# Weight tiles padded from 4,096 to 4,160 bytes in a partition, in a kernel of chunked scan, gated and squared-ReLU layers

## The chip, the cores and the metric

The kernel runs on one core of a Trainium2 chip. The metric is the device time of one execution in microseconds (us). Five engines work on their own instruction lists: TensorE (PE for matmuls, PEld for loads of the stationary operand), VectorE (DVE), ScalarE (ACT), GpSimd (POOL) and SyncE (SP, which issues most DMAs here). They share SBUF, a memory of 128 partitions; a tile is a piece of it that starts at the same byte address in each partition.

## The reference

Three layers follow one another on 3,072 tokens (4 batches of 768) of width 256.

```
for c in range(nc):                       # scan: 8 heads of 32, state 16, chunks
    L  = exp(cum_i - cum_j) * causal
    y[c] = (C B^T * L) x + (C state) * exp(cum)
    state = exp(sum la) * state + sum_j B_j x_j * decay_from_j
x = y as 3072 x 256
g = x @ w_gate; val = x @ w_val           # 256 x 1536 each
x = (silu(g) * val) @ w_out               # 1536 x 256
h = x @ w_in                              # 256 x 2048
out = (relu(h) ** 2) @ w_out2             # 2048 x 256
```

The weights come in as 64-bit numbers and are turned into 32-bit ones on the chip.

## The kernel before, in words

Nearly every product is taken three times: each operand is split into a high and a low part in a rounded 32-bit format (fp32r), and hi·hi, hi·lo and lo·hi are added in PSUM. So a matrix product of two 128-row halves is six matmuls for a front (L791: `g`, `v` and `h`, with weights stationary and the activations `xh_all`, `xl_all` moving) and six for a back (L905, L977: `acc`, with weights stationary and the activation's parts `p` moving). In the last 512 tokens of the third layer the roles are exchanged (L986: 128 x 128 pieces of `p` are stationary, 256 columns of the weights move). A few early products are taken once in full 32 bits instead, from the unsplit weights `v` and the activations `xf` or `t`.

A `Unit` (L382) stands for 1,024 columns of weights. `load` brings them by DMA into `raw`; ACT, DVE and POOL make the 32-bit value `v` (`mag` L441, `share` L447, `sign` L456, `clamp` L462, `shift` L466), then ACT writes the high part `hi` (`top`, L472) and POOL or DVE the low part `lo` (`rest`, L476). `v`, `hi` and `lo` are tiles of 128 x 1,024 words, so 4,096 bytes in a partition. Those of the first two layers and of the last four units of the third come from the pool `w` of 20 tiles (L188); the first four units of the third layer use room that the scan has given up (the pools `xf`, `tr`, `L`, `ab`, L1105).

The order of all work is written out beforehand: `Graph.order` (L51) walks the tables in `PLAN["seq"]`, one list for each engine, and only the costs and tables there decide it, no address. `new` (L225) takes a tile from a pool when an operation that needs it is issued.

The pools lie in SBUF one behind another, in the order in which they are opened: fixed tiles (among them `xh_all`, `xl_all`, `xa`, `mt`), then `w`, `raw`, `tmp` (the tiles `t` and `o`), `p`, `tr`, `L`, `ab`, `xf`, `st`. In the built program `w` begins at byte 73,856 of a partition. Below, a tile's *place* is its byte address less whole multiples of 1,024. All 20 tiles of `w` begin at place 128, and so do `xh_all`, `xl_all`, `raw`, `t`, `p`, the tiles of `tr`, `L`, `ab`, and `xf`. An operand of a matmul is a piece of a tile: a stationary one of 128 words (512 bytes) begins at place 128 or 640, since pieces follow each other by 512 bytes.

Of the kernel before, what the change touches and what calls it, by code (L numbers as in the profile page):

```python
# [141 lines left out]
def kernel(  # L142
# [23 lines left out]
    P = 128  # L166
# [8 lines left out]
    for b in range(NB):  # L175
        t = 0
        while t < S:
            n = min(Q, S - t)
# [10 lines left out]
    tp = {  # L189
        k: ctx.enter_context(  # L190
            tc.tile_pool(name=k, bufs=v, space=PSUM) if k.startswith("ps") else tc.tile_pool(name=k, bufs=v)
        )
        for k, v in pools.items()
    }
# [30 lines left out]
    def new(buf, shape, dtype, tag=None):  # L225
        n = 1
        for d in shape[1:]:
            n *= d
        if buf.pool in ("L", "ab") and n < 1024:

            t = tp[buf.pool].tile([P, 1024], dtype, tag=buf.pool, name=tag or buf.pool)[:, :n]
            buf.t = t.rearrange("p (a b) -> p a b", a=shape[1]) if len(shape) == 3 else t
        else:
            buf.t = tp[buf.pool].tile(shape, dtype, tag=buf.pool, name=tag or buf.pool)
        if buf.pool == "ps" and fills:


            t = buf.t.rearrange("p a b -> p (a b)") if len(shape) == 3 else buf.t
            t = t[:, : min(n, 256)]
            for _ in range(fills.pop()):  # L240
                nc.tensor.matmul(t, idle[:, : shape[0]], idle[:, : t.shape[-1]], start=True, stop=True)  # L241
        return buf.t
# [139 lines left out]
    class Unit:  # L382
# [37 lines left out]
        def load(self, raw, s, src):  # L420
            if raw.t is None:
                new(raw, [P, 2, 1024], I32)
            w, rows, j = src
            if rows:
                v = w[256 * j : 256 * j + 256, :].rearrange("(i p) f -> p i f", p=P)
            else:
                v = w[:, 512 * j : 512 * j + 512].rearrange("(k p) f -> p k f", p=P)
            nc.sync.dma_start(out=raw.t[:, s].rearrange("p (i f) -> p i f", i=2), in_=v)
# [8 lines left out]
        def mag(self, raw, c):  # L437

            if self.v.t is None:
                new(self.v, [P, 1024], F32, "v")  # L440
            nc.scalar.activation(self.part(c), self.words(raw, c)[1].bitcast(F32), AF.Abs, scale=65536.0)  # L441
# [28 lines left out]
        def top(self):  # L470
            new(self.hi, [P, 1024], F32R, "hi")
            nc.scalar.activation(self.hi.t, self.v.t, AF.Copy)  # L472
# [594 lines left out]
    for i, (j, c0, c1, exact) in enumerate(PLAN["cells"]):  # L1067
        ti, o = (0, c0 * Q) if c0 < 3 else (1, c0 * Q - cut)
        n = min(c1 * Q, S) - c0 * Q
# [55 lines left out]
    with tc.manual_schedule():  # L1125
        for op in order:
            fills.clear()
            if op.eng == "PE":
                if op.start < PLAN["warm"]:
                    free = max([last] + [o.start + o.took + 250 for o in op.after if o is not None])  # L1130
                    gap = op.start - free
                    n = (gap - COLD) / 110 + COLD / 216 if free < 1200 else gap / 105
# [153 lines left out]
```

## Time and profile before

| | before |
|---|---|
| median of 2 runs | 627.29 us (627.07 and 627.5) |
| profiled execution, its own time | 627.6 us |
| its span, first to last instruction | 625.9 us |
| PE busy | 619.8 us (99%), 3,682 matmuls |
| DVE busy | 424.6 us (68%) |
| ACT busy | 335.2 us (54%) |
| POOL busy | 99.4 us (16%) |
| mean granted clock of TensorE | 0.999 |

The profile is of one execution. "Busy" is time in which an engine has an instruction in flight. Matmuls overlap their neighbours, and the end of one is modelled: a 512-column matmul is listed with 389 ns, while the next starts 227 ns after it. The distance from start to start is therefore what a matmul costs in a stream, and it is read from the chain of work or from the order of time. A span of x matmuls in the chain of work, divided by x, gives it.

### The profile page before, as it was taken

The numbers are of one execution on the slowest core, as the hardware profiler recorded it, in microseconds if no ns is written. First come the engines' busy times: TensorE is split into PE (matmuls) and PEld (weight loads), VectorE is DVE, ScalarE is ACT, GpSimd is POOL, SyncE is SP. The second block draws the span as 40 slices with busy tenths as digits, with TensorE's granted clock in tenths as the row PEclk, the third lists the DMA queues.
The fourth block names the chain that finished last, engine by engine and source line by source line (L and its number), as shares of the span: only waits on it lengthen the run. The fifth ranks groups of instructions, "written<-read, shape, count | busy, mean of one in ns | idle before, by whom it ended". The sixth has DMA issues, their size and how long they took to land.

```text
span 625.9 us, 9674 instructions
## 1 busy us (share of the span) xinstructions
PE 619.8 (99%) x3682; PEld 525.1 (84%) x3682; DVE 424.6 (68%) x668; ACT 335.2 (54%) x615; POOL 99.4 (16%) x130
## 2 busy tenths in 40 slices
PE   8999999999999999999999999999999999999997
PEld 6889999998878787878888888888888888888897
DVE  7897888877876866883688985454545554545543
ACT  6898985455443535542476564444444444444443
POOL 2425513313121231211113310000000000000000
PEclk9999999999999999999999999999999999999999
DMA  8879975756656555640224200010010100200101
GB/s 185 212 191 228 209 151 93 132 110 124 135 96 132 99 102 118 148 137 33 68 68 135 68 1 0 1 34 1 9 26 1 35 2 0 35 0 1 34 1 36
DMA packets 153855, 49.85 MB, mean 80 GB/s; under 512 B 141648, under 2 KB 142160, under 8 KB 153808
## 3 DMA queue, kind: packets, MB, share of 16 engines
q1 hardware_dynamic: 153248, 48.87, 35.4%
q8 instruction: 29, 0.48, 0.3%
q10 hardware_dynamic: 560, 0.36, 0.2%
q14 instruction: 18, 0.15, 0.1%
HBM read 34.96 MB, written 3.25 MB: 61 GB/s over the span
## 4 chain that ended last, share of the span: by engine, by line
PE 98%; DMA 1%; DVE 0%; SPq 0%; issue 0%; DVEq 0%
PE h L791 21%; PE g L791 18%; PE acc L977 17%; PE acc L905 16%; PE v L791 14%; PE acc L986 4%; PE ys L727 3%; PE cb L688 2%; PE cb L679 1%; PE ab L616 1%; DMA dv<-in_a_dram 1%; PE trb L529 0%; PE g L241 0%; PE cb L241 0%; PE turn L766 0%; PE ab L241 0%
## 5 line engine op out<-in xcount | busy, mean ns | idle before, releaser
L967 DVE TENSOR_TENSOR p<-t,p 128x512 fp32r<-128x512 f32 x96 | 68.2, 713 | 65.2 <-ACT p L963 65.2
L963 ACT ACTIVATE p<-t 128x512 fp32r<-128x512 f32 x96 | 60.6, 633 | 75.9 <-PE acc L977 53.3
L960 DVE TENSOR_TENSOR t<-t 128x512 f32<-128x512 f32 x96 | 66.2, 691 | 51.6 <-ACT t L957 51.6
L977 PE MATMUL acc<-p,hi 128*128 128x512 f32 x320 | 98.6, 389 | 0.0
L957 ACT ACTIVATE t<-h 128x512 f32<-128x512 f32 x96 | 57.4, 598 | 66.1 <-PE h L791 63.2
L905 PE MATMUL acc<-p,hi 128*128 128x512 f32 (+3 forms) x320 | 90.2, 366 | 0.0
L855 ACT ACTIVATE t<-g 128x512 f32<-128x512 f32 (+5 forms) x88 | 44.8, 516 | 71.9 <-PE g L791 63.9
L791 PE MATMUL h<-xh_all,hi 128*128 128x512 f32 x192 | 74.8, 390 | 0.0
L791 PE MATMUL h<-xl_all,hi 128*128 128x512 f32 x192 | 74.8, 390 | 0.0
L791 PE MATMUL h<-xh_all,lo 128*128 128x512 f32 x192 | 74.7, 389 | 0.0
L878 DVE TENSOR_TENSOR p<-t,p 128x512 fp32r<-128x512 f32 (+3 forms) x80 | 57.4, 727 | 21.0 <-ACT p L873 20.4
L873 ACT ACTIVATE p<-t 128x512 fp32r<-128x512 f32 (+3 forms) x80 | 45.4, 572 | 47.2 <-DVE t L858 38.6
L977 PEld LDWEIGHTS acc<-p,hi 128*128 128x128 f32 x320 | 60.1, 188 | 12.5
L858 DVE TENSOR_TENSOR t<-t,v 128x512 f32<-128x512 f32 (+2 forms) x68 | 43.7, 647 | 36.0 <-PE v L791 26.8
L791 PE MATMUL g<-xh_all,hi 128*128 128x512 f32 (+3 forms) x184 | 65.3, 355 | 0.0
L791 PE MATMUL g<-xl_all,hi 128*128 128x512 f32 (+3 forms) x184 | 64.6, 351 | 0.0
L791 PE MATMUL g<-xh_all,lo 128*128 128x512 f32 (+3 forms) x184 | 64.6, 351 | 0.0
L905 PEld LDWEIGHTS acc<-p,hi 128*128 128x128 f32 x320 | 57.1, 189 | 7.3
L977 PE MATMUL acc<-p,lo 128*128 128x512 f32 x160 | 62.2, 389 | 0.0
L905 PE MATMUL acc<-p,lo 128*128 128x512 f32 (+3 forms) x160 | 57.9, 362 | 0.0
L791 PE MATMUL v<-xh_all,hi 128*128 128x512 f32 (+2 forms) x136 | 51.2, 377 | 0.0
L791 PE MATMUL v<-xl_all,hi 128*128 128x512 f32 (+2 forms) x136 | 51.0, 375 | 0.0
(108 smaller groups left out, 1071.7 us busy)
## 6 DMA issues: line engine op xcount, KB each, us to landing
ab<-decay SPq DMA_DIRECT2D x23, 452.0 KB, 4.2
raw<-in_moe_w_out_dram SPq DMA_DIRECT2D x14, 512.0 KB, 5.5
raw<-in_moe_w_in_dram SPq DMA_DIRECT2D x8, 512.0 KB, 3.8
raw<-in_moe_w_val_dram SPq DMA_DIRECT2D x6, 512.0 KB, 5.2
raw<-in_moe_w_gate_dram SPq DMA_DIRECT2D x6, 512.0 KB, 5.4
xa<-in_x_dram SPq DMA_DIRECT2D x24, 112.0 KB, 3.0
out_dram<-o SPq DMA_DIRECT2D x40, 64.0 KB, 1.9
bc<-in_B_dram SPq DMA_DIRECT2D x18, 56.0 KB, 2.9
```

The source lines that it names most:

```text
L791: nc.tensor.matmul(ps, l, r, start=(i == 0), stop=(i == len(terms) - 1))
L855: nc.scalar.activation(t[:, :n], gg(), AF.Silu)
L858: nc.vector.tensor_tensor(tb.t[:, :n], tb.t[:, :n], vv(), op=ALU.mult)
L873: nc.scalar.activation(p[:, 0, :n], tb.t[:, :n], AF.Copy)
L878: e.tensor_tensor(p[:, 1, :n], tb.t[:, :n], p[:, 0, :n].bitcast(F32), op=ALU.subtract)
L905: nc.tensor.matmul(ps, l, r, start=bank not in done_f, stop=f == NF - 1, skip_group_check=True,)
L957: nc.scalar.activation(new(tb, [P, TN], F32, "t"), ph.t, AF.Relu)
L960: nc.vector.tensor_tensor(tb.t, tb.t, tb.t, op=ALU.mult)
L963: nc.scalar.activation(new(pb, [P, 2, TN], F32R, "p")[:, 0, :], tb.t, AF.Copy)
L967: e.tensor_tensor(pb.t[:, 1, :], tb.t, pb.t[:, 0, :].bitcast(F32), op=ALU.subtract)
L977: nc.tensor.matmul(acc[-1 - i][m], l.t[:, w], pb.t[:, r, :], start=(f == 0 and s == 0), stop=(f == NF2 - 1 and s == 2),)
L986: nc.tensor.matmul(acc[-1 - i][q][:, :256], pb.t[:, l, tk], r, start=(f == 0 and s == 0), stop=(f == NF2 - 1 and s == 2),)
```

## The change

A tile of pool `w` is taken with 1,040 words instead of 1,024, and the last 16 words (64 bytes) are cut off again. Each tile still has 1,024 words in use, at a distance of 4,160 bytes from the next one.

```diff
@@ new(buf, shape, dtype, tag=None) @@
             t = tp[buf.pool].tile([P, 1024], dtype, tag=buf.pool, name=tag or buf.pool)[:, :n]
             buf.t = t.rearrange("p (a b) -> p a b", a=shape[1]) if len(shape) == 3 else t
+        elif buf.pool == "w":
+            buf.t = tp["w"].tile([P, 1040], dtype, tag="w", name=tag or "w")[:, :n]
         else:
             buf.t = tp[buf.pool].tile(shape, dtype, tag=buf.pool, name=tag or buf.pool)
```

The two added lines move the line numbers behind them by two (L977 becomes L979). On every engine the list of instructions is otherwise the same row for row, in the same order, with the same tile numbers and sizes: no instruction, no DMA and no wait is added, removed or moved. Only addresses differ. The tiles of `w` begin at 73,856 + 4,160·i, so at places 128, 192, 256 and so on in steps of 64 bytes. These are 16 places for 20 tiles: the last four stand at the places of the first four. Everything behind `w` (`raw`, `t`, `o`, `p`, `tr`, `L`, `ab`, `xf`, `st`) lies 1,280 bytes higher, so at place 384 where it was at 128. What lies ahead of `w` (`xh_all`, `xl_all`, `xa`, `mt` and the other fixed tiles) stays.

Of the 2,688 matmuls in fp32r, 1,968 take a stationary operand from a tile of `w`, and 96 a moving one. 1,068 of the 1,968 take it from tiles that begin at an odd multiple of 64 bytes after the change: 756 of them with 512 moving columns, 112 with 432, 88 with 336 and 112 with 256.

## Rows read from the trace of the kernel before

**Rows 1.** The page's head: the span, and busy time of PE.

```profile
span 625.9 us, 9674 instructions
PE 619.8 (99%) x3682; PEld 525.1 (84%) x3682; DVE 424.6 (68%) x668; ACT 335.2 (54%) x615; POOL 99.4 (16%) x130
```

**Rows 2.** PE by stretches: from:to, length, busy time (instructions), granted clock, DMA.

```profile
0.00:25.00 25.00, 22.19 (x228) 1.00 0.87 208
25.00:626.00 601.00, 597.62 (x3456) 1.00 0.34 74
```

**Rows 3.** What PE waited for: us in total, times, longest.

```profile
PE ab L616 <- DVE dv L279: 1.7, 1, 1.7
PE ab L241 <- DVE idle L223: 1.1, 1, 1.1
```

**Rows 4.** The chain that ended last, in order: start, length, what.

```profile
20.26 0.88 PE g L791 x8
...
29.47 2.27 PE g L791 x12
...
119.88 7.26 PE g L791 x60
...
403.51 1.36 PE acc L977 x6
404.87 1.36 PE h L791 x6
...
588.67 1.43 PE acc L986 x12
```

**Rows 5.** Groups of PE: line, operation, output<-inputs, shapes, count | busy, mean ns | idle.

```profile
L977 PE MATMUL acc<-p,hi 128*128 128x512 f32 x320 | 98.6, 389 | 0.0
L905 PE MATMUL acc<-p,hi 128*128 128x512 f32 (+3 forms) x320 | 90.2, 366 | 0.0
L791 PE MATMUL h<-xh_all,hi 128*128 128x512 f32 x192 | 74.8, 390 | 0.0
L791 PE MATMUL g<-xh_all,hi 128*128 128x512 f32 (+3 forms) x184 | 65.3, 355 | 0.0
L791 PE MATMUL v<-xh_all,hi 128*128 128x512 f32 (+2 forms) x136 | 51.2, 377 | 0.0
L986 PE MATMUL acc<-hi,p 128*128 128x256 f32 x128 | 25.1, 282 | 0.0
```

**Rows 6.** PE in order of time: start, length, line, operation, tiles, shape, count.

```profile
82.31 0.32 PE L791 MATMUL g<-xh_all,hi 128*128 128x336 f32 x1
...
83.25 0.47 PE L905 MATMUL acc<-p,hi 128*128 128x336 f32 x2
...
97.25 0.55 PE L905 MATMUL acc<-p,hi 128*128 128x432 f32 x2
...
98.43 0.35 PE L791 MATMUL g<-xh_all,hi 128*128 128x432 f32 x1
...
99.60 0.36 PE L791 MATMUL v<-xh_all,hi 128*128 128x432 f32 x1
...
174.36 0.57 PE L688 MATMUL cb<-bct 128*128 128x112 bf16 x8
174.75 0.47 PE L791 MATMUL g<-xh_all,hi 128*128 128x512 f32 x1
```

**Rows 7.** Loads of stationary operands by line: ns min/median/max, first and last start, forms.

```profile
L977 PEld LDWEIGHTS acc<-p,hi x320: 187/188/188, 366.4 to 580.8; 128*128 128x128 f32 x160
L688 PEld LDWEIGHTS <-bct x168: 95/98/101, 62.0 to 281.4; 128*128 128x128 bf16 x168
```

**Rows 8.** Two lines that write at seven places: same columns as rows 7.

```profile
L747 ACT ACTIVATE xh_all<-ys x28: 303/352/461, 16.1 to 286.4; 128x224 fp32r<-128x224 f32 x24, 128x192 fp32r<-128x192 f32 x4
L750 DVE TENSOR_TENSOR xl_all<-ys,xh_all x28: 345/382/393, 21.0 to 286.7; 128x224 fp32r<-128x224 f32 x24, 128x192 fp32r<-128x192 f32 x4
```

**Rows 9.** What POOL waited for before the low parts: us, times, longest.

```profile
POOL lo L476 <- ACT hi L472: 80.4, 9, 19.4
```

## Prediction

> **What bounds the kernel now.** I read the page's head first. PE is busy for 619.8 of 625.9 us, DVE for 424.6 and ACT for 335.2 [rows 1]. Busy time of PE alone says little, since its matmuls overlap, so the stretches come next: from 25 us to the end PE has work in flight for 597.6 of 601.0 us, at a granted clock of 1.00, which is the 2.4 GHz level [rows 2]. The list of waits then shows how little PE is held up: its two waits together are 2.8 us, both in the first 8 us and both on DVE work that has nothing to do with weights [rows 3]. The chain of work that ended last is a row of matmul groups that follow each other without a gap: six with 512 columns take 1.36 us, so 226.7 ns each, whether they are fronts or backs [rows 4]. So the time is the sum of the matmuls' distances from start to start. An edit counts if it changes that distance, or if it delays another engine so far that PE has to wait.
>
> **The price of a matmul.** A column takes 1/2.4 GHz = 0.4167 ns, so 512 columns take 213.3 ns, and the row's 226.7 ns hold 13.3 ns more. With 256 columns the distance is 7.26 us / 60 = 121 ns for fronts and 1.43 us / 12 = 119 ns for the exchanged backs [rows 4]; less 106.7 ns for the columns, that is 12 to 14 ns. The surplus is the same at every width, one amount for each matmul. In bf16 it is smaller: eight matmuls of 112 columns take 174.75 − 174.36 = 0.39 us [rows 6], 48.8 ns each, 2.1 ns over the 46.7 ns of the columns. The fp32r matmuls are 480 at L977, 480 at L905, 576 for h, 552 for g, 408 for v and 192 at L986, together 2,688 (the rows show one of each kind; a `hi` row of acc stands beside a `lo` row half as long, and each front row beside two others as long) [rows 5]. The surplus beyond the bf16 one, 13.3 − 2.1 = 11.2 ns, is 30.1 us in all. That is the only amount on the path that addresses could give back.
>
> **The change, part by part.** It removes and adds no instruction, wait or DMA and moves none, so the terms are prices of places.
>
> *Weights read as stationary operands from 16 places (1,968 matmuls).* Before, such an operand begins at place 128 or 640. The row of L977 holds both, since pieces of a tile follow each other by 512 bytes, and its 320 loads take 187 to 188 ns without exception [rows 7]; its groups and those of h take 1.36 us at either. So a move by 512 bytes is worth nothing. The distance between where the weights begin and where the moving columns begin could matter instead of the place. It takes other values too: the second token tile begins at token 336, so its moving columns from `xh_all` begin at place 448, and the distance to the weights is 192 or 704 bytes instead of 0 or 512. Six such fronts of 432 columns take 99.60 − 98.43 = 1.17 us, 195.0 ns each; six backs of 432 columns, whose moving `p` begins at place 128, take 98.43 − 97.25 = 1.18 us, 196.7 ns each [rows 6]. The one with shifted places is no slower and no faster within the 1.7 ns that a rounded row can hide. Both are 15 to 17 ns over their columns, and a 336-column group beside them, all at place 128 or 640, is 83.25 − 82.31 = 0.94 us, 156.7 ns each and 16.7 ns over: what is a little dearer there belongs to the stretch, not to the place. I take 0 for this term, since these rows are the nearest: the same engine, the same format, other places. For the ends I take what rounding leaves, 1.7 ns × 1,968 = 3.3 us either way.
>
> The Trainium skill ("TensorE: Matmul & The Clock Gate", section "Part 2: What happens when you issue a matmul") says that TensorE has two independent read ports, one for the streamed operand and one for the weight load, and that loading the next weights takes no read bandwidth from the running matmul. That speaks against any gain from this change, and the 187 to 188 ns agree with it, though they show two places and not sixteen.
>
> *Weights as moving operands (96 matmuls of L986), and `p`, `xf`, `tr`, `L`, `ab` at place 384 instead of 128.* The moving operand at 448 against 128 has just been priced at 0 to 1.7 ns. The other 720 fp32r matmuls see such shifts only; 0 with 1.2 us as an end either way, which I count as covered by the first term's.
>
> *Writes by ACT, DVE and POOL into `hi`, `lo` and `v` at new places.* The nearest rows are L747 and L750, which write chunks of `xh_all` and `xl_all` that begin 448 bytes apart, at seven places that are all multiples of 64. On DVE the 28 instructions take 345 to 393 ns with 382 in the middle, the shortest being the four smaller ones; on ACT 303 to 461 with 352 in the middle [rows 8]. So places cost these engines little if anything. If they did, it would be hidden: from 25 us on PE waits for none of them [rows 2, 3], and POOL itself stands idle 80.4 us waiting for high parts before it makes low ones [rows 9]. If a write took 100 ns longer, PE would not see it; without that cover a dozen of them would cost 1 us.
>
> *DMAs into `raw`, `ab`, `bcs`.* Their size and number stay, and the start shifts by a multiple of 256 bytes. PE's longest wait is for `dv` [rows 3], which does not move.
>
> **The sum:** 0, with ends of −3.3 and +3.3 us. The profiled execution took 627.6 us, 1.7 more than its span and 0.3 more than the median of the runs; I forecast that median, **627.3 us**, with 624.0 to 630.6 as this case's own range. About 2% (12.5 us) is what a measurement of this kernel can tell from no change.
>
> **The rivals.**
>
> *Faster: the surplus is a collision.* Weights and moving columns both begin at place 128, the load of the next weights starts with the matmul that streams, and both read words of the same place in step. If that makes the 11.2 ns, spreading the tiles over 16 places would give them back for the 2,064 matmuls that read a tile of `w`: 23.1 us, so 604.2 us; for all 2,688 it would be 597.2. For it: the surplus is constant, as 512 bytes of weights for each matmul would make it, and smaller in bf16 with half the bytes. Against it: 432 columns at 448 and at 128 cost the same [rows 6], and so do stationary pieces at 128 and 640 [rows 7]. The point from which it decides is 12.5 us / 2,064 = 6.1 ns for each. The same page of the Trainium skill, section "Back-to-back issue gap", gives N/2.4 + 2.5 ns for a warm isolated matmul; by that rule 512 columns would take 216 ns and these matmuls have 11 ns to give. The row of bf16 agrees with it and the fp32r rows do not; nothing in the trace ties the difference to a place. Chance 0.04.
>
> *Slower: a weight load from an odd multiple of 64 bytes takes twice as long.* None of the 20 tiles begins at one before, and 1,068 fp32r loads do after. The load itself is 188 ns long, but loads overlap: eight full 32-bit matmuls of 112 columns, each with a 128-column load, follow each other in 0.88 us, 110 ns each, though their columns need only half of the 2.27 us / 12 = 189 ns of 224 columns, that is 95 [rows 4]. So I estimate 110 ns for what a load needs for itself. Doubled it is 220 ns: hidden under 512 columns (226.7), but over the 197 ns of 432 columns by 23, over the 155 of 336 by 65 and over the 120 of 256 by 100. 112 × 23 + 88 × 65 + 112 × 100 ns = 19.5 us, so 646.8 us. It passes 2% from some 88 ns of added load time. For it: no row has a 128-word load from such a place. Against it: moving columns from place 448, an odd multiple of 64, cost nothing more. Chance 0.03.
>
> *The change does not spread as it says.* It does in part: 16 places, not 20, and 624 matmuls of the third layer take their weights from tiles that only move together. This would change the gain of the first rival, not the forecast.
>
> **How the numbers follow.** The forecast has 0.93, the two rivals 0.04 and 0.03; inside the forecast nothing passes 2%. Both rivals may be left outside a range that is to hold 8 in 10, so the range is the forecast's own, 624.0 to 630.6. Chances: faster by over 2% 0.04, within 2% 0.93, slower by over 2% 0.03.
>
> **What would show it.** In the profile of the changed kernel, groups of six with 512 columns should still take 1.36 us, twelve of L986 1.43 us, and the loads of the backs 187 to 188 ns at every tile. PE should have no wait on `hi`, `lo` or `v`. The prediction is wrong if the six take 1.30 us (the surplus is gone), or if the six stay but the groups of 256 and 336 columns grow (the load paces them), or if a wait of PE on a weight tile appears.

## The result, and the profile after

The changed kernel takes 635.99 us (635.57 and 636.41) against 627.29: a recorded ratio of 1.0124, with a 95% interval of 1.0107 to 1.0142 (the two medians alone give 1.0139). That is within 2%, as forecast, but it is a clear loss, of 8.7 us by the medians, where the forecast was none, and it lies outside the range of 624.0 to 630.6.

The head of the page after, to be read against [rows 1], and PE by two stretches, against [rows 2]:

```profile
span 634.7 us, 9674 instructions
PE 627.7 (99%) x3682; PEld 525.0 (83%) x3682; DVE 426.3 (67%) x668; ACT 336.7 (53%) x615; POOL 98.9 (16%) x130
```

```profile
0.00:25.00 25.00, 21.27 (x213) 0.86 0.85 204
25.00:635.00 610.00, 606.38 (x3473) 1.00 0.33 73
```

The span is 8.8 us longer, and so is PE's busy time by 7.9, with the same 3,682 matmuls. The other engines are busy for the same time within 2 us, so the work of none of them grew by more than 0.5%. From 25 us on PE still has work in flight nearly all the time, 606.4 of 610.0 us, at a granted clock of 1.00. Its waits, against [rows 3], are again short and early:

```profile
PE ab L618 <- DVE dv L281: 1.5, 1, 1.5
PE ab L243 <- DVE idle L223: 1.1, 1, 1.1
PE trb L531 <- DMA eb<-in_B_dram: 1.0, 1, 1.0
```

The wait for `eb`, whose tile did not move, and the lower granted clock of 0.86 in the first 25 us I take for this execution's own: the other run of the changed kernel had a mean clock of 1.000 and a span of 633.9 us, and ahead256 below, which costs nothing, has the same wait of 1.0 us. Executions of the kernel before with a mean clock of 1.000, recorded beside the experiments, spanned 626.5 to 627.3 us, so at a like clock the loss is 6.6 to 7.4 us. The wait and the clock put the first 32-bit front 1.6 us later (21.84 below against 20.26 in [rows 4]). The rest comes matmul by matmul, in most stretches but not in all. The chain of the kernel after, to be read against [rows 4]:

```profile
21.84 0.88 PE g L793 x8
...
121.46 7.12 PE g L793 x60
...
404.02 1.40 PE acc L979 x6
405.42 1.39 PE h L793 x6
406.80 1.40 PE acc L979 x6
408.20 1.39 PE h L793 x6
409.59 1.38 PE acc L979 x6
410.97 1.38 PE h L793 x6
412.36 1.37 PE acc L979 x6
413.73 1.36 PE h L793 x6
415.09 1.36 PE acc L979 x6
...
591.84 1.43 PE acc L988 x12
```

Six matmuls of 512 columns take up to 1.40 us here where they took 1.36, that is 233 ns each instead of 226.7. They are at 1.36 again from 413.73 us on, where fronts and backs both read weights from tiles at place 384, 0 or 256 bytes away from those of the moving operands by 1,024; the longer ones before read weights at places that are 64 or 192 over a multiple of 256, or follow such a group. The widths behave differently: sixty 256-column fronts take 7.12 us instead of 7.26, twelve of L988 the same 1.43. The fronts between those twelves take 1.39 us in both kernels, although in the kernel before all operands there stand at one place by 256 bytes. Of the kernel before:

```profile
590.10 1.39 PE h L791 x6
591.49 1.43 PE acc L986 x12
```

Set start against start for every matmul whose successor has the same width, and with steps that differ by over 40 ns left out, the 512-column ones lost 7.6 us, the 256-column ones won 0.6, and 336 and 432 columns changed by less than 0.1. With the 1.6 us of the start that is 8.6 of the 8.8.

The loads' own records do not show it. Of the kernel after, against the first of [rows 7]:

```profile
L979 PEld LDWEIGHTS acc<-p,hi x320: 187/188/192, 371.9 to 589.6; 128*128 128x128 f32 x160
```

The median is still 188 ns. From the first of these loads to the last it takes 217.7 us, from 371.9 to 589.6, against 214.4 before, so 3.3 us of the loss fall into this stretch of the third layer.

### The profile page after: what moved, and what is told of

Read it like the earlier page. It is cut to its first block, busy times and chain, and to the rows that moved or that the text cites. A ratio compares the mean times of both kernels' runs of the same rounds, so it can differ in the third digit from the quotient of the medians.

```text
span 634.7 us, 9674 instructions
## 1 busy us (share of the span) xinstructions
PE 627.7 (99%) x3682; PEld 525.0 (83%) x3682; DVE 426.3 (67%) x668; ACT 336.7 (53%) x615; POOL 98.9 (16%) x130
## 4 chain that ended last, share of the span: by engine, by line
PE 98%; DMA 1%; SPq 0%; DVE 0%; issue 0%
PE h L793 21%; PE g L793 18%; PE acc L979 17%; PE acc L907 16%; PE v L793 14%; PE acc L988 4%; PE ys L729 2%; PE cb L690 2%; PE cb L681 1%; DMA eb<-in_B_dram 1%; PE ab L618 1%; PE trb L531 0%; PE cb L243 0%; PE g L243 0%; PE ab L243 0%; PE turn L768 0%
## 5 line engine op out<-in xcount | busy, mean ns | idle before, releaser
L979 PE MATMUL acc<-p,hi 128*128 128x512 f32 x320 | 99.5, 392 | 0.0
L979 PEld LDWEIGHTS acc<-p,hi 128*128 128x128 f32 x320 | 60.1, 188 | 13.5
L979 PE MATMUL acc<-p,lo 128*128 128x512 f32 x160 | 62.7, 392 | 0.0
L793 PE MATMUL v<-xh_all,lo 128*128 128x512 f32 (+2 forms) x136 | 51.6, 379 | 0.0
```

Source lines behind the costliest of these rows:

```text
L793: nc.tensor.matmul(ps, l, r, start=(i == 0), stop=(i == len(terms) - 1))
L979: nc.tensor.matmul(acc[-1 - i][m], l.t[:, w], pb.t[:, r, :], start=(f == 0 and s == 0), stop=(f == NF2 - 1 and s == 2),)
```

## The experiments

All of them start from the kernel before; none but the last four changes an instruction. "Distance" below is the byte address where a matmul's stationary operand begins less that of its moving operand, and only its remainder by 256 is given. In the kernel before every 512-column matmul has distance 0.

| kernel | fronts / backs of layer 3 | us | ratio to before, 95% |
|---|---|---|---|
| gap1280 | 0 / 0 | 628.09 | 0.9999, 0.9989 to 1.0009 |
| ahead64 | 64 / 0 | 636.21 | 1.0125, 1.0110 to 1.0140 |
| all64 | 0 / 0 | 628.34 | 0.9998, 0.9989 to 1.0008 |
| ahead128 | 128 / 0 | 634.68 | 1.0105, 1.0090 to 1.0120 |
| p64 | 0 or 64 / 0 or 192 | 634.00 | 1.0094, 1.0077 to 1.0111 |
| ahead192 | 192 / 0 | 634.02 | 1.0097, 1.0076 to 1.0117 |
| ahead32 | 32 / 0 | 637.90 | 1.0158, 1.0135 to 1.0181 |
| ahead256 | 0 / 0 | 627.83 | 0.9997, 0.9984 to 1.0010 |
| ahead160 | 160 / 0 | 638.70 | 1.0176, 1.0146 to 1.0207 |
| ahead224 | 224 / 0 | 638.53 | 1.0174, 1.0144 to 1.0203 |
| dist16 | 16 / 0 | 635.74 | 1.0129, 1.0100 to 1.0159 |
| dist240 | 240 / 0 | 635.51 | 1.0126, 1.0096 to 1.0155 |

The kernel before had medians of 628.26 beside the first four, 628.68 beside the next four and 627.50 beside the last four.

### gap1280: the shift behind w alone

```diff
-    pools = dict(w=20, raw=2, ...)
+    pools = dict(w=20, gap=1, raw=2, ...)
...
+    tp["gap"].tile([P, 320], F32, name="gap")
+    del pools["gap"]
```

> The tiles of w stay at a distance of 4,096 bytes and at byte 73,856; an unused tile of 1,280 bytes stands between w and raw, so that everything behind w lies where the change puts it. Theory 1 (what costs is the distance between where the stationary and the moving operand begin, less whole multiples of 256 bytes): every such distance stays 0, so 627 to 628 us and 1.36 us for six matmuls of 512 columns. Theory 2 (the stationary operand's own address, less multiples of 256, must be 128): the same, 627 to 628. Rival (the shift of p, L, ab, tr and the DMA targets behind w costs the time, not the tiles of w): 634 to 636 us, with the longer groups in L977.

Measured 628.09 us, a ratio of 0.9999. So moving `raw`, `p`, `L`, `ab`, `tr` and `xf` by 1,280 bytes costs nothing, and the loss comes from the tiles of `w`. Its chain:

```profile
441.68 1.36 PE acc L979 x6
443.04 1.36 PE h L793 x6
```

### ahead64, all64, ahead128: one move against another

```diff
     dv_all = const.tile([P, NCB, Q + 1], F32, name="dv")     # the last of the fixed tiles before w
+    gap = const.tile([P, 16], F32, name="gap")               # ahead64; 32 words in ahead128
```

```diff
+    gap = const.tile([P, 16], F32, name="gap")        # all64
     xh_all = const.tile([P, 2, T], F32R, name="xh_all")
```

> Weights unpadded, 4,096 bytes apart; an unused tile of 64 bytes stands ahead of w, so that w and all behind it (p too) move by 64 bytes against xh_all and xl_all. Theory 1 (distance between stationary and moving operand, mod 256): the 1,152 fronts of 512 columns, whose moving operand is xh_all or xl_all, cost 3.5 to 6.5 ns more each, as the groups of the change with their weights at 64 or 192 mod 256 did, the 768 backs, whose moving operand p has moved along, nothing: 631 to 635 us, six fronts 1.38 to 1.40 us and six backs 1.36. Theory 2 (the stationary operand's own address must be 128 mod 256): fronts and backs both longer, 634 to 640 us. Theory 3 (what costs is that consecutive stationary operands, hi and lo, stand at different places): nothing changes, 627 to 628 us.

> An unused tile of 64 bytes stands ahead of everything, so that all operands, xh_all and xl_all too, begin at 192 mod 256 and no distance between two of them changes. Theory 1 (distance): 627 to 628 us, 1.36 us for six of 512 columns. Theory 2 (own address must be 128 mod 256): 634 to 640 us, six in 1.38 to 1.40 us. Theory 3 (hi and lo at different places): 627 to 628 us.

> As with 64 bytes ahead of w, but 128. Theory 1 (distance mod 256): the fronts of 512 columns are at a distance of 128, which the change has with weights at 0 mod 256; those groups were 5.6 to 6.8 ns a matmul longer there, so 1,152 x 6 ns = 7 us, 633 to 636 us, backs unchanged. If the period is 128 and not 256 bytes: 627 to 628. Theory 2: fronts and backs longer, 637 to 641. Theory 3: 627 to 628 us.

Moving weights by 64 bytes against `xh_all` costs as much as the whole change, 636.21 us, and moving everything together by the same 64 bytes costs nothing, 628.34. In ahead64 the weights still stand 4,096 bytes apart, and hi and lo of a unit at the same place by 256, so theory 3 cannot explain this loss; whether unlike places of hi and lo add to it in the changed kernel was not tried alone. In all64 the stationary operand's own address is the one that cost time in ahead64, so theory 2 falls. What counts is how the addresses stand to each other. The chains, ahead64 first and then all64:

```profile
440.25 1.40 PE h L792 x6
441.65 1.38 PE acc L978 x6
443.03 1.40 PE h L792 x6
444.43 1.38 PE acc L978 x6
```

```profile
441.28 1.36 PE h L792 x6
442.64 1.36 PE acc L978 x6
```

One expectation of theory 1 was wrong: the backs of ahead64, at distance 0, take 1.38 us and not 1.36, and the time lies 1.2 us above the 631 to 635 that it asked for. From start to start, the six steps from a back's first matmul on are 226, 236, 228, 233, 231 and 226 ns, to within 1 ns in all of the 70 pairs of a front and a back that I took from the third layer: they begin disturbed by the fronts ahead and end undisturbed. Where a second group of backs follows the first, three times in the third layer, its steps are 226 to 227 ns. So here a group at distance 0 needs about six matmuls to come back into step. In ahead128 fronts take 1.39 and backs 1.37.

### p64: the moving operand of the backs moved instead

```diff
-    pools = dict(..., raw=2, tmp=4, p=3, ...)
+    pools = dict(..., raw=2, tmp=4, gap=1, p=3, ...)
...
+    tp["gap"].tile([P, 16], F32, name="gap")
+    del pools["gap"]
```

> Weights unpadded, w where it was; an unused tile of 64 bytes stands between tmp and p, so that p, tr, L, ab and xf begin at 192 mod 256 and w, xh_all and xl_all stay at 128. In the third layer the units 0 to 3 have their weights in xf, tr, L, ab (now 192) and the units 4 to 7 in w (128). Theory 1 (distance between stationary and moving operand, mod 256) asks for a crossing: with units 0 to 3 the six fronts take 1.39 to 1.40 us and the six backs settle to 1.36; with units 4 to 7 the fronts settle to 1.36 and the backs take 1.38 to 1.40; the fronts of the second layer (w against xh_all) 1.36, its backs longer. With 288 fronts and 528 backs of 512 columns at 4 to 6 ns, 3.3 to 5 us, and as much as half of that again for groups that follow a disturbed one: 631 to 635 us. Rival (only the address of the stationary operand counts, distance or not): with units 4 to 7 neither is longer, and with units 0 to 3 both are.

Measured 634.00 us. The second layer shows what theory 1 asked for. Its chain in p64, where fronts (`g`, `v`) have distance 0 and backs (`acc`) 192:

```profile
312.75 1.39 PE acc L907 x6
314.14 1.39 PE g L793 x6
315.53 1.39 PE acc L907 x6
316.92 1.39 PE v L793 x6
318.31 1.39 PE acc L907 x6
319.69 1.39 PE g L793 x6
321.08 1.38 PE v L793 x6
322.46 1.36 PE g L793 x6
323.82 1.36 PE v L793 x6
```

A back takes 1.39 us, the fronts right behind it too, and the third front in a row is at 1.36 again. The weights stand where they stood before, at 128 by 256, in all these groups, backs and fronts, so the rival falls. The crossing that I expected in the third layer did not come: there groups of both kinds take 1.37 to 1.40. In one stretch both are at distance 0, the fronts with weights and `xh_all` at 128 and the backs with weights and `p` at 192, yet neither settles:

```profile
426.29 1.38 PE acc L979 x6
427.67 1.38 PE h L793 x6
429.05 1.38 PE acc L979 x6
430.44 1.38 PE h L793 x6
```

So distance 0 inside each matmul is not enough. Each group of six also stands 64 bytes away from the one before, and that is what is left to keep the train out of step. What holds in all runs so far: the low price needs all operands of consecutive groups at the same place by 256. (The backs of dist16, below, are an exception.)

### ahead192, ahead32, ahead256, ahead160, ahead224, dist16, dist240: which distances are free

```diff
     dv_all = const.tile([P, NCB, Q + 1], F32, name="dv")
+    gap = const.tile([P, 8], F32, name="gap")     # 32 bytes; 40, 48, 56 and 64 words for 160 to 256
```

```diff
-    xh_all = const.tile([P, 2, T], F32R, name="xh_all")
+    xh_all = const.tile([P, 2 * T + 64], F32R, name="xh_all")[:, 60:60 + 2 * T].rearrange(
+        "p (a t) -> p a t", a=2)          # dist16; 4:4 + 2 * T in dist240, xl_all alike
```

> 192 bytes ahead of w, so the fronts are at a distance of 192, which is -64. Theory 1 with a symmetric price: as with 64 bytes, 635 to 637 us, fronts of the third layer 233 ns each. Theory 1 with a price that follows the sign: between 627 and 634.

> 32 bytes ahead of w, so the fronts are at a distance of 32 mod 256. Theory 1 says only that the distance decides: if the price grows with the distance, half of what 64 bytes cost, 630 to 633 us; if every distance but 0 costs the same, 634 to 637 us. A distance at which 512-column matmuls come closer than 226.7 ns would show a gain, under 627 us; nothing seen so far points to it.

> 256 bytes ahead of w, so the fronts are at a distance of 256. Theory 1 with a period of 256 bytes: 627 to 628.5 us, all groups of 512 columns 1.36 us. With a period of 512 or 1,024 bytes: 633 to 637 us.

> 160 bytes ahead of w: fronts at distance 160 mod 256, backs at 0. From the fronts that follow fronts in the runs so far (32: 6.6, 64: 6.6, 128: 6.5, 192: 2.2 ns a matmul over 226.7), between 128 and 192: 3 to 6 ns, and half as much for the backs behind them: 633 to 636 us. If every distance but 0 costs alike: 635 to 638.

> 224 bytes ahead of w: fronts at distance 224, that is -32. If the price falls off from 192 on, 0 to 2 ns a front, 628 to 632 us; if it goes on falling below zero, under 627 us, which would be a layout faster than the kernel before. If the price depends on the size of the distance alone, as at 32: 636 to 638 us.

> xh_all and xl_all get 64 unused words each and begin 240 bytes later in their tiles, so that fronts are at a distance of 16 bytes, four words; backs stay at 0. If any distance but 0 costs as much as 32 does: 635 to 638 us. If the price grows with the distance: 627 to 632 us.

> xh_all and xl_all begin 16 bytes later in their tiles, so that fronts are at a distance of 240, that is -16; backs stay at 0. If only distance 0 is free: 632 to 638 us. If the price falls towards 256: 627 to 630 us. Under 627 us if a small negative distance brings matmuls closer.

Only the distance of 256 is free, at 627.83 us; all others cost 5 to 11 us, 16 bytes as much as 64. Three times lie 0.5 to 0.9 us above the highest that was expected: ahead32, ahead160 and ahead224. Neither a price that grows with the distance nor one that is symmetric about 0 holds. From start to start a front and its back in the third layer take 2,720 ns before, 2,760 at 16 bytes, 2,787 at 32, 2,780 at 64, 2,767 at 128, 2,793 at 160, 2,773 at 192, 2,787 at 224 and 2,773 at 240. So 64 and 192 differ, and so do 16 and 240, while 32 and 224 are alike. No distance brings 512-column matmuls closer than 226.7 ns on average, so none of these is a faster kernel. In dist16 the backs take 1.36 us right behind fronts that take 1.40: there the disturbance is not passed on, and no run shows why. The chains of ahead256 and then of dist16:

```profile
440.68 1.36 PE h L792 x6
442.04 1.36 PE acc L978 x6
```

```profile
440.64 1.40 PE h L791 x6
442.04 1.36 PE acc L977 x6
```

### h448, h432 and both with 64 bytes ahead: the width

In the fronts of the third layer the first of six matmuls has 512 columns and the other five have m, 448 or 432; the columns beyond m miss these terms.

```diff
-            product(h, terms)
+            for s, (l, r) in enumerate(terms):
+                m = 448 if s else TN
+                nc.tensor.matmul(h[:, :m], l, r[:, :m], start=s == 0, stop=s == 5)
```

> Layout of before (distance 0). In the fronts of the third layer the first of six matmuls has 512 columns, the other five have 448 (1,792 bytes, seven times 256); the last 64 columns miss these five terms. Width theory (at distance 0 the low price needs widths that are whole multiples of 64 columns, 256 bytes): inside the six the narrow ones follow each other in 186.7 + 13.3 = 200 ns. Rival (512 and 256 are special for another reason): 202 to 205, as 432 columns at 195 to 197 were.

> The same at distance 0 with 432 columns (1,728 bytes, 6.75 times 256) in five of six matmuls; the last 80 columns miss these terms. Width theory: 195 to 198 ns each with a spread of several ns from matmul to matmul, 15 to 18 over the columns, though ScalarE, VectorE and GpSimd have less to do here than in the stretch where 432 was read before. Rival (what was dearer at 432 belonged to the early stretch, as the prediction had it): 180 + 13.3 = 193.3 ns, all alike.

> The 448-column fronts with 64 bytes ahead of w, so at distance 64; the same terms left out. Width theory: the price of the distance shows as at 512 columns, 4 to 7 ns: 204 to 207 ns each. Rival (only 512 columns pay for a distance): 200 to 202.

> The 432-column fronts at distance 64; the same terms left out. Width theory: no more than at distance 0, 195 to 198 ns each, since at 432 the low price is lost anyway. Rival (432 pays for the distance too): 199 to 203.

One run each: 615.49, 614.95, 621.36 and 617.92 us, beside 628.58 of the kernel before. Their chains, in the order h448, h432, h448_64, h432_64:

```profile
441.24 1.24 PE h L956 x6
442.48 1.36 PE acc L979 x6
```

```profile
441.27 1.21 PE h L956 x6
442.48 1.39 PE acc L979 x6
```

```profile
440.73 1.24 PE h L957 x6
441.96 1.39 PE acc L980 x6
```

```profile
441.94 1.21 PE h L957 x6
443.15 1.38 PE acc L980 x6
```

Taken as pairs of six and six, a front with its back has seven matmuls of 512 columns and five of m. With m = 448 their columns take 5,824 × 0.4167 ns = 2.427 us, with m = 432 2.393 us. From start to start the pairs take 2.600, 2.600, 2.627 and 2.593 us, so the surplus for a matmul is 14.4 ns at 448 and distance 0, 17.2 at 432 and distance 0, 16.7 at 448 and 64, and 16.7 at 432 and 64. For 512 columns it is 13.3 in the kernel before and (2.78 − 2.56) / 12 = 18.3 in ahead64. So the distance costs 5 ns at 512 columns, 2.2 at 448 and nothing at 432, where the low price is lost at distance 0 already. The 432-column fronts of the second layer, which all runs have, agree: they follow each other in 195.5 ns on average in the kernel before, at distance 192, in 196.0 at 0 (ahead64), 195.0 at 64 (ahead128) and 194.8 at 128 (ahead192). The backs say the same: behind 448 columns they stay at 1.36 us, behind 432 they take 1.39 although every matmul there has distance 0.

The width theory got only part of this right. At 432 columns it did: the narrow ones take 197 ns on average in h432, spread from 192 to 203, and 196 in h432_64. It asked for 200 ns at 448 and distance 0; the timeline of h448 has the five narrow ones from 441.30 to 442.31 us, 202 ns each, which is the rival's number. At distance 64 it asked for 204 to 207 in the fronts, and they take 200 there, with the loss in the backs. The price falls on whatever matmul comes later in the train, so single groups mislead and only the sum over a repeating piece is to be read.

## Why the prediction was wrong

**What bounds the kernel: right.** The time is the sum of distances from start to start, PE waits for nobody after the first microseconds, and, apart from 1.6 us at the start of the profiled execution, the loss is in those distances.

**The step that failed** is the first term, "weights read as stationary operands from 16 places", taken at 0 with ends of 3.3 us. It measured about +7 us: 7.6 lost at 512 columns and 0.6 won at 256. Two readings carried the zero, and neither could show the price. The row of L977 with places 128 and 640 [rows 7] compares two that are 512 bytes apart, twice the period of 256, so it is one place. The fronts of 432 columns, at a distance of 192 or 704 bytes, which is 192 by 256, do stand at a distance that costs the kernel 5.3 us when its 512-column fronts have it (ahead192); they showed nothing against the backs of 432 columns because at that width the low price is lost at any distance tried (h432 against h432_64, and these very fronts at 0, 64 and 128 bytes). The prediction saw the sign of it, 15 to 17 ns of surplus instead of 13.3 [rows 6], and put it down to the stretch. h432 speaks against that: 17.2 ns at 440 us, where the surplus is 13.3 in the kernel before. "The surplus is the same at every width" had been read at 512 and 256 columns alone. And the trace of the kernel before did hold a dearer state at 512 columns, the fronts from 587 us on that take 1.39 us for six among the 256-column groups of L986. That row would have said that a distance of 226.7 ns can be lost without any wait. The signs named for being wrong had no place for it either: six that take longer while the loads stay at 188 ns.

**The ends** came from what rounding hides in rows that turned out not to see the effect. The bound for 512 columns at a distance that the trace never had at 512 columns was open, and the 432-column surplus itself, 2 to 4 ns above the 512-column one, would have been the nearest row for it: 1,968 times 2 to 4 ns is 4 to 8 us. That it comes near the 7 us measured would have been luck, since h432 has this surplus at distance 0 too.

**The other terms: right.** DMA targets, writes by ACT, DVE and POOL, `p` and the late homes by 256 bytes more: gap1280 moves these alone and costs nothing, and the 96 matmuls that stream weights are among the twelves of L988, which stay at 1.43 us. The new places of `hi`, `lo` and `v` as targets of writes were not tried alone; the busy times of the engines stay within 0.5%, and no wait of PE on them appears.

**The faster rival** had a collision between the two streams in it, and places do matter, but the other way round: equal places are the cheapest of all those tried, and 13.3 ns is what is left then. **The slower rival** had the sign and the wrong mechanism. A load that takes twice as long would have hit 256-column matmuls first; those became 2 ns faster (7.12 us for sixty), the loads are 188 ns as before, and 512 columns paid.

The Trainium skill ("TensorE: Matmul & The Clock Gate", "Part 2: What happens when you issue a matmul") says that loading the next weights takes no read bandwidth from the running matmul. The loads' records, 188 ns in both kernels, do not speak against it, but they cannot show a price either. The runs show that where the weights stand relative to the streamed operand changes the matmul's distance by some 5 ns; whether that is read bandwidth or something else is not shown.

**What stays open.** That the effect sits between the stationary and the moving reads is shown by ahead64 against all64, and by dist16 and dist240, which move `xh_all` and `xl_all` alone against all else by 256. Why its period is 256 bytes, why a train of matmuls needs six or more to come back into step in most runs and none in dist16, why 336 and 432 columns and the fronts beside L986 are dearer at distance 0, and why 256 columns gain a little, is not: the runs show a timing that repeats, not what is behind it.

## What to carry to other kernels

A kernel bound by back-to-back matmuls can depend on where its operands begin. Here the 512-column distances were alike to the nanosecond, at 226.7 ns, with all operands at one place by 256 bytes, and each of the eight other distances tried cost 5 to 11 us. So a first choice for padding is a multiple of 256 (shifts by 256 and 1,280 bytes were free; 256 bytes of padding for each tile were not tried). Before a row is used to price a new address, ask whether it is itself in the cheap state: rows that are already a few ns dearer, or spread, cannot show the price of leaving it.

## What the runs showed of the hardware

- For fp32r matmuls of 512 columns the distance from start to start is 226.7 ns when stationary and moving operands of all groups begin at the same place by 256 bytes, wherever that is (128 in the kernel before, 192 in all64), and 231 to 234 on average over six in fronts of the third layer at any of the eight other distances tried (16 to 240 bytes). Among the 256-column groups of L986 it is 232 ns at one place by 256 too (1.39 us for six).
- A disturbed group mostly passes it on: groups at distance 0 behind one take 1.37 to 1.39 us for six and need one or two groups to come back to 1.36 (p64, ahead64). In dist16 they are at 1.36 at once.
- The timing then repeats exactly with the pattern of the program. Twelve matmuls, a front and a back, take from start to start 2,720 ns before, 2,780 in ahead64, 2,767 in ahead128, 2,787 in ahead32, 2,760 in dist16, and 2,600 in both h448 and h432: whole multiples, within a nanosecond, of 6.67 ns, the time of 16 columns.
- Moving `w` by 64 bytes brings 256-column fronts from 120 to 114 ns on average, as 512-column ones go from 227 to 233. A layout that gives the 144 fronts of 256 columns this and leaves the rest in step would be worth an estimated 144 × 6 ns = 0.9 us; it was not tried.
